# Attention followed by a gated projection on one core: heads paired as h and h+4, fewer loads, and projections issued as pairs of 128x64 column tiles

## The chip, the cores and the metric

The kernel runs on 1 core of one Trainium2 chip. The metric is the device time of one execution in microseconds (us), as the median of several executions. A profile of one execution shows every instruction of the five engines: TensorE (PE, whose weight loads are listed apart as PEld), VectorE (DVE), ScalarE (ACT), GpSimd (POOL) and SyncE (SP), which issues most of the transfers (DMAs).

## The reference

The inputs are q, k and v of shape 8 x 8 x 576 x 64 (batches, heads, tokens, head dimension, float32), a threshold tau, w_in (512 x 2048) and w_out (2048 x 512).

```python
scores = scale * np.matmul(q, k.transpose(0, 1, 3, 2))        # scale = 1/8
thresh = np.max(scores, axis=-1, keepdims=True) - tau
scores = np.where(scores >= thresh, scores, -1000000000.0)
attn   = softmax(scores)
x      = np.matmul(attn, v)          # heads side by side: 4608 tokens x 512
h      = x @ w_in
g      = h * np.clip(h + 3.0, 0.0, 6.0) / 6.0
out    = g @ w_out
```

## The kernel before, in words

**Slots.** Two heads make a pair, two pairs a quad; a batch has 8 heads, so two quads. A quad is done in nine slots: four slots of 128 queries for each pair, and a ninth (slot 8) with the last 64 queries of both pairs. 16 quads give 144 slots, numbered n. A slot computes for two heads at once a 128 x 576 table of scores, its row maximum, a mask, an exponential, its row sum, and the normalized probabilities in bf16, which are transposed into the tile pT (or pR for slot 8) by a DMA on SP, for the first slots by PE.

**The order is written out by hand.** Every engine runs its instructions in the order in which the loop over n (line 539) emits them. From slot 22 on (N1), slots come in twos, and PE does this:

- even slot: the first projection `mm1` (eight matmuls of 256 columns, line 394, or four of 512, line 389, for the rows that are left over of two batches), then eight matmuls of the second projection `mm2_part` (line 428, 512 columns);
- odd slot: `mm1` again, then, where the table `products` has one, a product of probabilities and v (`av`, lines 359 and 362: five steps, each a pair of matmuls), then the scores of two slots to come (line 295).

DVE does in every slot two maxima (line 310, which also copy the scores out of PSUM), a reciprocal (330) and the gate (417). In odd slots it also has the ReLU (404), the copy of the `av` result (370 or 380), every second time the copy of an output tile (436), and in some the transposition of a pair of q (245) or k (251). ACT does two masks (322) and two exponentials (327) in every slot, and the ReLU in even slots (402). POOL does the bias of the mask (317), the normalization (335), and issues the loads that change type.

**Shapes on PE.** A matmul of the scores contracts over 64 rows, since a head has 64 dimensions: the two heads of a pair lie on partitions 0 to 63 and 64 to 127 and use the two halves of the array's rows at once (in the profile 64\*128, rows by columns). A step of `av` is two matmuls of 128 rows by 64 columns (128\*64), one for each head, which write partitions 0 to 63 and 64 to 127 of the result. Projections and transpositions use the whole array (128\*128).

**Pairs and loads.** A pair is heads 2i and 2i+1. From batch 2 on (NB = 2) q and k are loaded by SP in blocks of 32 tokens by 32 dimensions, each piece 128 bytes, so that DVE can transpose them in 32 x 32 blocks (`blocks_q`, `blocks_k`, four DMAs for one pair). Of k the first 512 tokens go that way. The last 64 keys of a quad are loaded apart (tile kr, line 127, by POOL from quad 5 on), transposed by PE in an even slot (`transpose_rest`, line 261) and copied from PSUM by ACT in the odd slot after it (line 226, two copies). In kT the two heads of a pair lie in different column order, which is why line 294 adds 64 \* (1 - a).

**v.** Key tokens sit on the partitions of vm: 128 partitions of four tokens for the first 512, and the last 64 tokens in vr, whose other half is zero. An `av` step c takes one of the four tokens of each partition; the fifth step takes vr.

Of the kernel before, what the change touches and what calls it, by code (L numbers as in the profile page):

```python
# [9 lines left out]
F32 = mybir.dt.float32  # L10
# [10 lines left out]
def kernel(  # L21
# [60 lines left out]

    def load_quad(quad):
        b, g = divmod(quad, 2)
        nat[quad] = (nat_pool.tile([P, 1152], F32, tag="nq", name="nq"),
                     nat_pool.tile([P, 4, 4, D], F32, tag="km", name="km"),
                     nat_pool.tile([P, 2 * D], F32, tag="kr", name="kr"))
        nq, km, kr = nat[quad]

        def main(dst, src, h, order, by=nc.sync):  # L90
            by.dma_start(out=dst[:, :, h, :], in_=src[b, 4 * g + h, 0:512, :].rearrange(order, t=4))

        def blocks_q(n, a, j):
            c = 32 * (2 * a + j)
            nc.sync.dma_start(out=nq[c:c + 32, n * S:(n + 1) * S].rearrange("p (k d) -> p k d", d=32),
                              in_=q[b, 4 * g + 2 * n + a, :, 32 * j:32 * j + 32].rearrange("(k r) d -> r k d", r=32))

        def blocks_k(n, a, j):
            c = 32 * (2 * a + j)
            nc.sync.dma_start(  # L100
                out=km[c:c + 32].rearrange("p t h d -> p (t h d)")[:, n * 512:(n + 1) * 512].rearrange(
                    "p (t m d) -> p t m d", t=4, d=32),
                in_=k[b, 4 * g + 2 * n + a, 0:512, 32 * j:32 * j + 32].rearrange("(m r t) d -> r t m d", r=32, t=4))

        def load_k(n):
            if b < NB:
                for a in range(2):
                    main(km, k, 2 * n + a, "(p t) d -> p t d", by=nc.scalar if quad == n == 0 else nc.sync)
            else:
                for a in range(2):  # L110
                    for j in range(2):
                        blocks_k(n, a, j)

        def load_q(n):
            if b < NB:
                for a in range(2):
                    main(nq[:, 0:1024].rearrange("p (t h d) -> p t h d", h=4, t=4), q, 2 * n + a, "(t p) d -> p t d")
            else:
                for a in range(2):
                    for j in range(2):  # L120
                        blocks_q(n, a, j)

        def rest():
            for dst, src in ((kr[:], k), (nq[:, 1024:1152], q))[0:2 if b < NB else 1]:
                for n in range(2):
                    by = nc.scalar if quad == 0 and src is k else nc.sync if quad < 5 else nc.gpsimd
                    by.dma_start(out=dst[64 * n:64 * n + 64, :].rearrange("p (h d) -> p h d", h=2),
                                 in_=src[b, 4 * g + 2 * n:4 * g + 2 * n + 2, 512:S, :].rearrange("h p d -> p h d"))

        def both():  # L130
            rest()
            load_k(1)

        if b < NB:
            loads.extend((lambda: load_k(0), lambda: load_q(0), rest, lambda: load_k(1), lambda: load_q(1)))
        else:
            loads.extend((lambda: load_q(0), lambda: load_k(0), lambda: load_q(1), both))

    def load_v(b):
        vm = v_pool.tile([P, H, 4 * D], BF16, tag="vm", name="vm")  # L140
        vr = vrs[b % 2]
        vsb[b] = (vm, vr)
        w = 4 if b < NB else 2
        mains = [lambda h=h: nc.gpsimd.dma_start(  # L144
            out=vm[:, h:h + w, :], in_=v[b, h:h + w, 0:512, :].rearrange("h (p t) d -> p h (t d)", t=4))
            for h in range(0, H, w)]
        rests = [lambda a=a: nc.gpsimd.dma_start(
            out=vr[a * 64:(a + 1) * 64, a, :, :],
            in_=v[b, :, 512:S, :].rearrange("(hp a) p d -> a p hp d", a=2)[a]) for a in range(2)]
        vcasts.extend(mains + rests if b < NB else mains[0:1] + rests + mains[1:])  # L150


    vrs = []
# [6 lines left out]
    w_out_sb = singles.tile([P, NI, d_model], BF16)  # L160

    def load_weights():
        for n4 in range(4):
            for ki in range(KI):
                casts.append(lambda n4=n4, ki=ki: nc.gpsimd.dma_start(
                    out=w_in_sb[:, ki, n4 * 512:(n4 + 1) * 512],
                    in_=moe_w_in[ki * P:(ki + 1) * P, n4 * 512:(n4 + 1) * 512]))
        for ni in range(NI):
            casts.append(lambda ni=ni: nc.gpsimd.dma_start(
                out=w_out_sb[:, ni, :], in_=moe_w_out[ni * P:(ni + 1) * P, :]))  # L170
# [76 lines left out]
    def transpose_k(pair):  # L247
        if not by_pe(pair):
            n = pair % 2
            km = nat[pair // 2][1][:].rearrange("p t h d -> p (t h d)")  # L250
            nc.vector.transpose(out=kT_of(pair)[:, 64:576], in_=km[:, n * 512:(n + 1) * 512])
            return None
        pb = main_pe(nat[pair // 2][1], pair)
        return lambda: copy_out(kT_of(pair)[:, 64:576], pb)

    def transpose_rest(quad, of_k=True, of_q=True):
        pb = bank()
        nq, _, kr = nat[quad]
        of_q = of_q and by_pe(2 * quad)
        if of_k:  # L260
            nc.tensor.transpose(pb[:, 0:P], kr[:], identf[:])
        if of_q:
            nc.tensor.transpose(pb[:, P:2 * P], nq[:, 1024:1152], identf[:])

        def evict():
            qT, kT = qkT[quad]
            both = pb.rearrange("p (w n t) -> p w n t", n=2, t=64)
            if of_q:
                nc.vector.tensor_copy(out=qT[:, :, 512:S], in_=both[:, 1])
            if of_k:  # L270
                copy_out(kT[0:64, :, S:S + 64], both[0:64, 0])
                copy_out(kT[64:P, :, 0:64], both[64:P, 0])
        return evict
# [9 lines left out]
    def scores(n):  # L283
# [4 lines left out]
        for group in [((a,), parts) for a in heads] if n in (1, 2) else [(heads, (part,)) for part in parts]:  # L288
            for i in range(2 if slot == 8 else 1):
                for a, (k0, w) in [(a, part) for part in group[1] for a in group[0]]:  # L290
                    pair = 2 * quad + (i if slot == 8 else slot // 4)
                    rows = slice(64 * i, 64 * i + 64) if slot == 8 else slice(0, P)
                    q0 = 512 if slot == 8 else slot % 4 * P
                    c0, kc = score_col(n, a) + k0, 64 * (1 - a) + k0
                    nc.tensor.matmul(ps_flat[rows, c0:c0 + w],  # L295
                                     qT_of(pair)[a * 64:(a + 1) * 64, q0:q0 + rows.stop - rows.start],
                                     kT_of(pair)[a * 64:(a + 1) * 64, kc:kc + w], start=True, stop=True)
# [56 lines left out]
    def av(pb, pair, pT, cols):  # L354
        b, hp = divmod(pair, NPAIR)
        vm, vr = vsb[b]
        for c in range(4):
            for a in range(2):
                nc.tensor.matmul(pb[a * 64:(a + 1) * 64, :], vm[:, 2 * hp + a, c * D:(c + 1) * D],  # L359
                                 pT[:, 5 * a + c, cols], start=(c == 0), stop=False)  # L360
        for a in range(2):
            nc.tensor.matmul(pb[a * 64:(a + 1) * 64, :], vr[:, a, hp, :], pT[:, 4, cols], start=False, stop=True)  # L362
# [19 lines left out]

    def mm1(item, hb=HB):
        b, ni, c0 = item
        if c0 is None:
            for ki in range(KI):
                nc.tensor.matmul(ps[:, hb, :], xR[b // 2][:, ki, :], w_in_sb[:, ki, ni * P:ni * P + 512],  # L389
                                 start=(ki == 0), stop=(ki == KI - 1))  # L390
        else:
            for n in range(2):
                for ki in range(KI):
                    nc.tensor.matmul(ps[:, hb, n * 256:(n + 1) * 256], w_in_sb[:, ki, (ni + n) * P:(ni + n + 1) * P],  # L394
                                     xT[b][:, ki, c0:c0 + 256], start=(ki == 0), stop=(ki == KI - 1))
        return ps[:, hb, :]


# [25 lines left out]
    def mm2_part(bb, mt, part, ob=OB):  # L424
        if part == 0:
            o_ps[0] = ps[:, ob, :]
        for ni in range(part * 4, part * 4 + 4):
            nc.tensor.matmul(o_ps[0], gbuf[:, ni, mt * P:(mt + 1) * P], w_out_sb[:, ni, :],  # L428
                             start=(ni == 0), stop=(ni == NI - 1))

    def mm2_out(bb, mt, on_act):
        osb = o_pool.tile([P, d_model], F32, tag="osb", name="osb")
# [66 lines left out]
    for quad in range(1, NQUAD):  # L499
        n0 = quad * NSLOT  # L500
        first_odd = n0 - 9 + quad % 2
        for i, (job, of) in enumerate((("q", 2 * quad), ("k", 2 * quad), ("rest", quad),
                                       ("q", 2 * quad + 1), ("k", 2 * quad + 1))):
            turn_at(n0 + ((-5, -5, -4, -2, -1) if quad == 1 else (-6, -5, -4, -2, -1))[i] if quad < 3 else
                    first_odd + (0, 2, 3, 4, 6)[i] if quad > 3 else first_odd + (0, 2, 3, 5, 7)[i], job, of)

# [32 lines left out]
    for n, sl in enumerate(queue):  # L539
# [111 lines left out]
        elif n not in (4, 12, 15, 18, 21) and not 23 < n < 30 and (n < 37 or n % 2 == 0):  # L651
            start(loads, 1)
        if n < 4 or 15 < n < 20 or n > 33:
            start(vcasts, 1 if n < N1 or n % 2 else 0)
        else:
            start(casts, 2 if n in (5, 8, 11, 14) or 21 < n < 28 else 1)
        prev = sl
# [87 lines left out]
```

## Time and profile before

| | |
|---|---|
| median of 3 runs | 513.19 us (512.69 to 513.75) |
| span of the profiled execution, first to last instruction | 511.0 us |
| mean granted TensorE clock | 0.999 |
| DVE busy | 442.8 us (87%) |
| ACT busy | 450.3 us (88%) |
| POOL busy | 298.6 us (58%) |
| transposition of k by DVE, 128x512 (line 251) | 24 times, 704 ns |
| transposition of the last keys by PE (line 261) | 15 times |
| copies of the last keys by ACT, 64x128 (line 226) | 24 times, 253 ns |
| loads of the last keys by POOL (line 127) | 22 times, 632 ns |
| loads of q and of k by SP in blocks | 96 and 96, 72 KB and 64 KB, 3.4 and 3.2 us to landing |

The profiled execution has no time of its own beside its span; the runs' median lies 2.2 us above the span, which is the time around the first and last instruction. A group of the profile is named by its line, engine, operation, what it writes and reads, and how often it ran. Instructions on one engine overlap a little, so the distance from one start to the next is shorter than the duration that the profile gives; both are used below and told apart. Idle time is put down to what released the engine ("issue" means that nothing that the profile shows was waited for).

### The profile page before, as it was taken

What the parts mean: (1) busy time and instruction counts of PE and PEld (TensorE: products, weight loads), DVE (VectorE), ACT (ScalarE), POOL (GpSimd) and SP (SyncE); (2) the same over time, 40 slices, a digit from 0 to 9 for tenths busy, and PEclk for the clock granted to TensorE, in tenths of its full rate; (3) what the DMA queues carried; (4) which work ended last, traced back from release to release, by engine and by line L of the source; (5) the groups of instructions that cost most, each with busy time, mean ns of one, the idle gap of its engine ahead of it and who ended that gap; (6) DMA issues with size and microseconds to landing.
All of it is one profiled execution on the core that took longest, in us unless ns stands there. A gap on an engine that the chain in (4) does not pass through costs nothing.

```text
span 511.0 us, 12107 instructions
## 1 busy us (share of the span) xinstructions
PE 503.4 (99%) x4132; PEld 319.8 (63%) x4132; DVE 442.8 (87%) x1127; ACT 450.3 (88%) x977; POOL 298.6 (58%) x539
## 2 busy tenths in 40 slices
PE   8999999999999999999999999999999999999997
PEld 7656566666655666666655666666655666667564
DVE  4788899989999999999999999999999999887251
ACT  4999999999999999999999999999999999987160
POOL 2788879666666756656565656666566755552000
PEclk9999999999999999999999999999999999999999
DMA  6998999989999999999899999999999996563132
GB/s 144 182 172 147 153 143 182 174 157 178 188 160 172 163 174 160 205 162 181 150 158 181 154 163 163 179 169 175 163 178 149 187 177 116 114 111 75 72 57 77
DMA packets 314318, 78.77 MB, mean 154 GB/s; under 512 B 296880, under 2 KB 309424, under 8 KB 314256
## 3 DMA queue, kind: packets, MB, share of 16 engines
q1 hardware_dynamic: 294464, 67.90, 78.0%
q0 software_dynamic: 18304, 9.64, 15.6%
q8 instruction: 32, 0.52, 0.4%
q10 hardware_dynamic: 1488, 0.46, 0.4%
q14 instruction: 30, 0.25, 0.2%
HBM read 36.70 MB, written 9.44 MB: 90 GB/s over the span
## 4 chain that ended last, share of the span: by engine, by line
PE 80%; DVE 4%; ACT 3%; issue 1%; DVEq 0%
PE ps L295 24%; PE ps L428 23%; PE ps L394 20%; PE ps L359 7%; PE ps L389 3%; DVE s L310 1%; PE ps L362 1%; ACT s L327 1%; ACT s L322 1%; DVE g L417 1%; DVE r L404 1%; PE ps L668 1%; ACT r L402 1%; PE ps L350 0%; DVE xT L370 0%
## 5 line engine op out<-in xcount | busy, mean ns | idle before, releaser
L335 POOL TENSOR_SCALAR pn<-s,rinv 128x576 bf16<-128x576 f32 x288 | 210.6, 743 | 19.4 <-issue 4.8
L310 DVE TENSOR_SCALAR_CACHE_REDUCE s<-ps 128x576 f32<-128x576 f32 x288 | 205.0, 748 | 13.4 <-POOL pn L335 5.1
L322 ACT ACTIVATE s<-s,bias 128x576 f32<-128x576 f32 x288 | 205.7, 762 | 3.6 <-POOL bias L317 3.2
L327 ACT ACTIVATE s<-s 128x576 f32<-128x576 f32 x288 | 192.5, 671 | 0.3
L295 PE MATMUL ps<-kT,qT 64*128 64x384 f32 (+7 forms) x1280 | 175.5, 419 | 2.1 <-DVE s L310 2.0
L295 PEld LDWEIGHTS ps<-kT,qT 64*128 64x128 f32 (+1 forms) x1280 | 103.7, 175 | 57.8 <-issue 15.6
L394 PE MATMUL ps<-xT,w_in_sb 128*128 128x256 bf16 x1024 | 131.0, 273 | 0.6 <-DVE g L417 0.5
L428 PE MATMUL ps<-w_out_sb,g 128*128 128x512 bf16 x560 | 130.7, 379 | 0.0
L394 PEld LDWEIGHTS <-w_in_sb 128*128 128x128 bf16 x1024 | 95.6, 98 | 40.3 <-issue 21.0
L317 POOL TENSOR_SCALAR bias<-m 128x2 f32<-128x2 f32 (+1 forms) x147 | 27.5, 187 | 148.4 <-DVE rinv L330 132.1
L417 DVE SCALAR_TENSOR_TENSOR g<-r,ps 128x512 bf16<-128x512 f32 x128 | 87.8, 687 | 13.6 <-ACT r L402 9.1
L428 PEld LDWEIGHTS <-g 128*128 128x128 bf16 x560 | 54.6, 98 | 55.0 <-issue 0.4
L402 ACT ACTIVATE r<-ps,three 128x512 f32<-128x512 f32 x81 | 55.4, 686 | 25.1 <-PE ps L394 20.2
L327 ACT ACTIVATION_READ_ACCUMULATOR s<-s 128x1 f32 x288 | 54.5, 189 | 0.0
L404 DVE TENSOR_SCALAR r<-ps 128x512 f32<-128x512 f32 x63 | 42.9, 681 | 0.0
L359 PE MATMUL ps<-pT,vm 128*64 128x256 bf16 (+1 forms) x480 | 39.1, 285 | 0.0
L359 PEld LDWEIGHTS <-vm 128*64 128x64 bf16 x736 | 27.2, 110 | 16.1 <-issue 14.7
L370 DVE CAST xT<-ps 128x256 bf16<-128x256 f32 (+1 forms) x60 | 26.2, 437 | 10.2 <-PE ps L362 10.2
L436 DVE TENSOR_SCALAR osb<-ps 128x512 f32<-128x512 f32 x31 | 20.8, 672 | 8.4 <-PE ps L428 8.4
L310 DVE DVE_READ_ACCUMULATOR s<-ps 128x1 f32 x288 | 23.9, 83 | 0.0
L330 DVE RECIPROCAL rinv<-rsum 128x2 f32<-128x2 f32 x144 | 23.0, 160 | 0.7 <-ACT s L327 0.6
L144 POOL DMA_DIRECT2D vm<-in_v_dram x28 | 21.4, 766 | 0.1
(60 smaller groups left out, 256.6 us busy)
## 6 DMA issues: line engine op xcount, KB each, us to landing
out_dram<-osb SPq DMA_DIRECT2D x31, 256.0 KB, 2.6
nq<-in_q_dram SPq DMA_DIRECT2D x96, 72.0 KB, 3.4
km<-in_k_dram SPq DMA_DIRECT2D x96, 64.0 KB, 3.2
vm<-in_v_dram POOLq DMA_DIRECT2D x24, 128.0 KB, 3.9
nq<-in_q_dram SPq DMA_DIRECT2D x16, 128.0 KB, 4.9
w_in_sb<-in_moe_w_in_dram POOLq DMA_DIRECT2D x16, 128.0 KB, 3.7
w_out_sb<-in_moe_w_out_dram POOLq DMA_DIRECT2D x16, 128.0 KB, 4.1
pT<-pn SPq DMA_TRANSPOSE x117, 3.8
```

The lines of the kernel that those rows point to most:

```text
L295: nc.tensor.matmul(ps_flat[rows, c0:c0 + w], qT_of(pair)[a * 64:(a + 1) * 64, q0:q0 + rows.stop - rows.start], kT_of(pair)[a * 64:(a + 1) ...
L310: nc.vector.tensor_scalar(out=sl.s[:, i, :], in0=ps_flat[:, c0:c0 + S], scalar1=1.0, scalar2=None, op0=Alu.mult, op1=Alu.max, accum_out=sl ...
L317: nc.gpsimd.tensor_scalar(out=sl.bias[:, of], in0=sl.m[:, of], scalar1=-scale, scalar2=tau, op0=Alu.mult, op1=Alu.add)
L322: nc.scalar.activation(out=s, in_=s, func=Act.Prelu, bias=sl.bias[:, i:i + 1], scale=scale, alpha=REJECT)
L327: nc.scalar.activation(out=s, in_=s, func=Act.Exp, accum_out=sl.rsum[:, i:i + 1])
L335: nc.gpsimd.tensor_scalar(out=pn[:, i, :], in0=sl.s[:, i, :], scalar1=sl.rinv[:, i:i + 1], scalar2=1.0, op0=Alu.mult, op1=Alu.mult)
L359: nc.tensor.matmul(pb[a * 64:(a + 1) * 64, :], vm[:, 2 * hp + a, c * D:(c + 1) * D], pT[:, 5 * a + c, cols], start=(c == 0), stop=False)
L394: nc.tensor.matmul(ps[:, hb, n * 256:(n + 1) * 256], w_in_sb[:, ki, (ni + n) * P:(ni + n + 1) * P], xT[b][:, ki, c0:c0 + 256], start=(ki = ...
L402: nc.scalar.activation(out=r, in_=hps, func=Act.Relu, bias=three[:])
L404: nc.vector.tensor_scalar(out=r, in0=hps, scalar1=3.0, scalar2=0.0, op0=Alu.add, op1=Alu.max)
L417: nc.vector.scalar_tensor_tensor(out=out, in0=r, scalar=6.0, in1=hps, op0=Alu.min, op1=Alu.mult)
L428: nc.tensor.matmul(o_ps[0], gbuf[:, ni, mt * P:(mt + 1) * P], w_out_sb[:, ni, :], start=(ni == 0), stop=(ni == NI - 1))
```

## The change

Four things change together.

1. A pair is now heads h and h+4 of a batch. Which head lies where in xT changes with it, and the rows of w_in are loaded in the matching order: 8 DMAs of 64 x 4 x 512 in place of 16 of 128 x 512.
2. From batch 2 on, one DMA brings the blocks of two heads: 48 and 48 DMAs in place of 96 and 96, with pieces of 128 bytes as before. k is loaded whole (576 tokens), so there is no separate load, PE transposition or ACT copy of the last keys for these 12 quads. Token t of k is placed so that the keys of both heads come out in the same column order; DVE's transposition of k becomes two instructions (5 and 4 blocks of 64 columns). v is loaded in the matching order of tokens, in the same number of DMAs.
3. Every matmul of the projections is issued as two of 128x64, one for each half of the result's partitions, in all slots but the last. After the loop they are whole again.
4. The loads of v are given out a little differently (one in each slot below 40).

```diff
-        def blocks_k(n, a, j):
-            c = 32 * (2 * a + j)
-            nc.sync.dma_start(
-                out=km[c:c + 32].rearrange("p t h d -> p (t h d)")[:, n * 512:(n + 1) * 512].rearrange(
-                    "p (t m d) -> p t m d", t=4, d=32),
-                in_=k[b, 4 * g + 2 * n + a, 0:512, 32 * j:32 * j + 32].rearrange("(m r t) d -> r t m d", r=32, t=4))
+        def blocks(dst, src, a, order, **sizes):
+            rows = src[b, 4 * a + 2 * g:4 * a + 2 * g + 2].rearrange("n t d -> (n t) d")
+            for j in range(2):
+                c = 32 * (2 * a + j)
+                nc.sync.dma_start(out=dst[c:c + 32].rearrange("p (k d) -> p k d", d=32) if len(sizes) == 1 else
+                                  dst[c:c + 32].rearrange("p (t x d) -> p t x d", d=32, t=9),
+                                  in_=rows[:, 32 * j:32 * j + 32].rearrange(order, **sizes))
...
-            loads.extend((lambda: load_q(0), lambda: load_k(0), lambda: load_q(1), both))
+            loads.extend((lambda: load_q(0), lambda: load_k(0), lambda: load_q(1), lambda: load_k(1)))
...
-            km = nat[pair // 2][1][:].rearrange("p t h d -> p (t h d)")
-            nc.vector.transpose(out=kT_of(pair)[:, 64:576], in_=km[:, n * 512:(n + 1) * 512])
+            rows = nat[pair // 2][1][:].rearrange("p (t n w) -> p t n w", t=9, n=2)[:, :, n, :]
+            out = kT_of(pair)
+            for u in range(2):
+                e = 5 - u
+                nc.vector.transpose(out=out[:, 0:640].rearrange("p (c u w) -> p c u w", u=2, w=64)[:, 0:e, u, :],
+                                    in_=rows[:, 5 * u:5 * u + e, :])
...
+    def half_columns(out, lhsT, rhs, start, stop):
+        w = 64 if now < len(queue) - 1 else P
+        for c in range(0, P, w):
+            nc.tensor.matmul(out[c:c + w], lhsT[:, c:c + w], rhs, start=start, stop=stop)
+
     def mm1(item, hb=HB):
...
-                    nc.tensor.matmul(ps[:, hb, n * 256:(n + 1) * 256], w_in_sb[:, ki, (ni + n) * P:(ni + n + 1) * P],
-                                     xT[b][:, ki, c0:c0 + 256], start=(ki == 0), stop=(ki == KI - 1))
+                    half_columns(ps[:, hb, n * 256:(n + 1) * 256], w_in_sb[:, ki, (ni + n) * P:(ni + n + 1) * P],
+                                 xT[b][:, ki, c0:c0 + 256], start=(ki == 0), stop=(ki == KI - 1))
...
-            nc.tensor.matmul(o_ps[0], gbuf[:, ni, mt * P:(mt + 1) * P], w_out_sb[:, ni, :],
-                             start=(ni == 0), stop=(ni == NI - 1))
+            half_columns(o_ps[0], gbuf[:, ni, mt * P:(mt + 1) * P], w_out_sb[:, ni, :],
+                         start=(ni == 0), stop=(ni == NI - 1))
...
+            if job == "rest" and quad // 2 >= NB:
+                continue
```

More of the change, by code (lines that the diff above doesn't have):

```diff
@@ L84, in load_quad, with main @@
         b, g = divmod(quad, 2)
-        nat[quad] = (nat_pool.tile([P, 1152], F32, tag="nq", name="nq"),
-                     nat_pool.tile([P, 4, 4, D], F32, tag="km", name="km"),
-                     nat_pool.tile([P, 2 * D], F32, tag="kr", name="kr"))
+        nat[quad] = (nat_pool.tile([P, 2 * S], F32, tag="nq", name="nq"),
+                     nat_pool.tile([P, 2 * S], F32, tag="km", name="km"),
+                     nat_pool.tile([P, 2 * D], F32, tag="kr", name="kr") if b < NB else None)
         nq, km, kr = nat[quad]
-        def main(dst, src, h, order, by=nc.sync):
-            by.dma_start(out=dst[:, :, h, :], in_=src[b, 4 * g + h, 0:512, :].rearrange(order, t=4))
-        def blocks_q(n, a, j):
-            c = 32 * (2 * a + j)
-            nc.sync.dma_start(out=nq[c:c + 32, n * S:(n + 1) * S].rearrange("p (k d) -> p k d", d=32),
-                              in_=q[b, 4 * g + 2 * n + a, :, 32 * j:32 * j + 32].rearrange("(k r) d -> r k d", r=32))
-        def blocks_k(n, a, j):
-            c = 32 * (2 * a + j)
-            nc.sync.dma_start(
-                out=km[c:c + 32].rearrange("p t h d -> p (t h d)")[:, n * 512:(n + 1) * 512].rearrange(
-                    "p (t m d) -> p t m d", t=4, d=32),
-                in_=k[b, 4 * g + 2 * n + a, 0:512, 32 * j:32 * j + 32].rearrange("(m r t) d -> r t m d", r=32, t=4))
+        def main(dst, src, n, a, order, by=nc.sync):
+            by.dma_start(out=dst[:, 0:1024].rearrange("p (t h d) -> p t h d", h=4, t=4)[:, :, 2 * n + a, :],
+                         in_=src[b, 4 * a + 2 * g + n, 0:512, :].rearrange(order, t=4))
+        def blocks(dst, src, a, order, **sizes):
[5 more added lines that the diff above has]
+                                  in_=rows[:, 32 * j:32 * j + 32].rearrange(order, **sizes))
         def load_k(n):
@@ L107, in load_k @@
                 for a in range(2):
-                    main(km, k, 2 * n + a, "(p t) d -> p t d", by=nc.scalar if quad == n == 0 else nc.sync)
+                    main(km, k, n, a, "(p t) d -> p t d", by=nc.scalar if quad == n == 0 else nc.sync)
             else:
-                for a in range(2):
-                    for j in range(2):
-                        blocks_k(n, a, j)
+                blocks(km, k, n, "(x r t) d -> r t x d", r=32, t=9)
         def load_q(n):
@@ L116, in load_q @@
                 for a in range(2):
-                    main(nq[:, 0:1024].rearrange("p (t h d) -> p t h d", h=4, t=4), q, 2 * n + a, "(t p) d -> p t d")
+                    main(nq, q, n, a, "(t p) d -> p t d")
             else:
-                for a in range(2):
-                    for j in range(2):
-                        blocks_q(n, a, j)
+                blocks(nq, q, n, "(k r) d -> r k d", r=32)
         def rest():
-            for dst, src in ((kr[:], k), (nq[:, 1024:1152], q))[0:2 if b < NB else 1]:
+            for dst, src in ((kr[:], k), (nq[:, 1024:1152], q)):
                 for n in range(2):
-                    by = nc.scalar if quad == 0 and src is k else nc.sync if quad < 5 else nc.gpsimd
+                    by = nc.scalar if quad == 0 and src is k else nc.sync
                     by.dma_start(out=dst[64 * n:64 * n + 64, :].rearrange("p (h d) -> p h d", h=2),
[L128 to L132, printed above, removed]
+                                 in_=src[b].rearrange("(a n) t d -> n a t d", a=2)[2 * g + n, :, 512:S, :].rearrange(
+                                     "a p d -> p a d"))
         if b < NB:
@@ L142, in load_v, with tokens @@
         vsb[b] = (vm, vr)
[L143 to L150, printed above, removed]
+        if b < NB:
+            mains = [lambda h=h: nc.gpsimd.dma_start(
+                out=vm[:, h:h + 4, :], in_=v[b, h:h + 4, 0:512, :].rearrange("h (p t) d -> p h (t d)", t=4))
+                for h in range(0, H, 4)]
+            rests = [lambda a=a: nc.gpsimd.dma_start(
+                out=vr[a * 64:(a + 1) * 64, a, :, :],
+                in_=v[b, 4 * a:4 * a + 4, 512:S, :].rearrange("h p d -> p h d")) for a in range(2)]
+        else:
+            def tokens(a, first, count):
+                return v[b, 4 * a:4 * a + 4].rearrange("h (p t) d -> p h (t d)", t=9)[
+                    :, :, first * D:(first + count) * D]
+            mains = [lambda a=a, u=u, first=first: nc.gpsimd.dma_start(
+                out=vm[64 * u:64 * u + 64, 4 * a:4 * a + 4, :], in_=tokens(a, first, 4))
+                for a, u, first in ((0, 0, 0), (0, 1, 5), (1, 0, 5), (1, 1, 1))]
+            rests = [lambda a=a: nc.gpsimd.dma_start(
+                out=vr[a * 64:(a + 1) * 64, a, :, :], in_=tokens(a, 4 * (1 - a), 1)) for a in range(2)]
+        vcasts.extend(mains + rests)
     vrs = []
@@ L162, in load_weights @@
     def load_weights():
+        rows = moe_w_in.rearrange("(a ki d) f -> a d ki f", a=2, ki=KI)
         for n4 in range(4):
[L164 to L167, printed above, removed]
+            for a in range(2):
+                casts.append(lambda n4=n4, a=a: nc.gpsimd.dma_start(
+                    out=w_in_sb[64 * a:64 * a + 64, :, n4 * 512:(n4 + 1) * 512],
+                    in_=rows[a, :, :, n4 * 512:(n4 + 1) * 512]))
+                casts.append(lambda: None)
         for ni in range(NI):
@@ L249, in transpose_k @@
             n = pair % 2
-            km = nat[pair // 2][1][:].rearrange("p t h d -> p (t h d)")
-            nc.vector.transpose(out=kT_of(pair)[:, 64:576], in_=km[:, n * 512:(n + 1) * 512])
+            rows = nat[pair // 2][1][:].rearrange("p (t n w) -> p t n w", t=9, n=2)[:, :, n, :]
[4 more added lines that the diff above has]
+                                    in_=rows[:, 5 * u:5 * u + e, :])
             return None
-        pb = main_pe(nat[pair // 2][1], pair)
+        pb = main_pe(nat[pair // 2][1][:, 0:1024].rearrange("p (t h d) -> p t h d", h=4, t=4), pair)
         return lambda: copy_out(kT_of(pair)[:, 64:576], pb)
@@ L258, in transpose_rest @@
         nq, _, kr = nat[quad]
-        of_q = of_q and by_pe(2 * quad)
         if of_k:
@@ L293, in scores @@
                     q0 = 512 if slot == 8 else slot % 4 * P
-                    c0, kc = score_col(n, a) + k0, 64 * (1 - a) + k0
+                    c0, kc = score_col(n, a) + k0, (64 * (1 - a) if by_pe(pair) else 0) + k0
                     nc.tensor.matmul(ps_flat[rows, c0:c0 + w],
@@ L358, in av @@
             for a in range(2):
-                nc.tensor.matmul(pb[a * 64:(a + 1) * 64, :], vm[:, 2 * hp + a, c * D:(c + 1) * D],
+                nc.tensor.matmul(pb[a * 64:(a + 1) * 64, :], vm[:, 4 * a + hp, c * D:(c + 1) * D],
                                  pT[:, 5 * a + c, cols], start=(c == 0), stop=False)
@@ L388, in mm1 @@
             for ki in range(KI):
-                nc.tensor.matmul(ps[:, hb, :], xR[b // 2][:, ki, :], w_in_sb[:, ki, ni * P:ni * P + 512],
-                                 start=(ki == 0), stop=(ki == KI - 1))
+                half_columns(ps[:, hb, :], xR[b // 2][:, ki, :], w_in_sb[:, ki, ni * P:ni * P + 512],
+                             start=(ki == 0), stop=(ki == KI - 1))
         else:
@@ L653 @@
         if n < 4 or 15 < n < 20 or n > 33:
-            start(vcasts, 1 if n < N1 or n % 2 else 0)
+            start(vcasts, 1 if n < 40 or n % 2 else 0)
         else:
```

## The prediction

> **What bounds the kernel now.** I read the busy times first, then the chain that ended last, then the order of time on PE in two slots.
>
> ```profile
> PE 503.4 (99%) x4132; PEld 319.8 (63%) x4132; DVE 442.8 (87%) x1127; ACT 450.3 (88%) x977; POOL 298.6 (58%) x539
> ...
> PE 80%; DVE 4%; ACT 3%; issue 1%; DVEq 0%
> ```
>
> PE is busy for all but 7.6 us and makes most of the chain. A busy PE need not be at its peak, so the distances between starts count. This is PE's timeline, start and length in us, from an even slot to the next scores:
>
> ```profile
> 314.75 1.05 PE L394 MATMUL ps<-xT,w_in_sb 128*128 128x256 bf16 x8
> 315.64 1.89 PE L428 MATMUL ps<-w_out_sb,g 128*128 128x512 bf16 x8
> 317.36 1.04 PE L394 MATMUL ps<-xT,w_in_sb 128*128 128x256 bf16 x8
> 318.33 0.63 PE L359 MATMUL ps<-pT,vm 128*64 128x256 bf16 x8
> 318.79 0.28 PE L362 MATMUL ps<-pT,vr 128*64 128x256 bf16 x2
> 319.00 0.59 PE L295 MATMUL ps<-kT,qT 64*128 64x384 f32 x2
> ```
>
> Eight L394 before L428 take 0.89; before L359 they take 0.97, and L362's one pair takes 0.21 up to the scores. With the starts in ns: 109.2 from one L394 to the next, but 202.4 from the last L394 to the first L359 (50 times, all within 1 ns), 308 in place of 209 from scores to L394, 202 in place of 105 from L362 to the scores. A change of array shape costs 93 to 99 ns each time, and waits for nothing. Two slots hold three such changes. The second view is an earlier `av`, its first start and then, from a view that begins inside it, its third pair:
>
> ```profile
> 311.94 0.63 PE L359 MATMUL ps<-pT,vm 128*64 128x256 bf16 x8
> 312.40 0.28 PE L362 MATMUL ps<-pT,vr 128*64 128x256 bf16 x2
> ```
>
> ```profile
> 312.18 0.39 PE L359 MATMUL ps<-pT,vm 128*64 128x256 bf16 x4
> ```
>
> Two pairs in 0.22 us from 312.18 to 312.40: a pair of 128x64 tiles takes 109.2 ns (105.8 to the next pair, 3.4 within it), as one 128x128 matmul does. The first two took 0.24: the first pair after a change of shape takes 133, 24 more (start to start, all `av` of 256 columns). For 512 columns a pair takes 216, the first 236; for 64 columns 32, the first 53.
>
> **The change, part by part.** The compiled order of the new kernel gives the counts: 1376 projection matmuls become pairs (872 of 256 columns, 504 of 512).
>
> 1. Projections and `av` have one shape now: 59 of 61 changes into `av` go. 59 x 93.2 = 5.50 us.
> 2. Those `av` no longer start cold: 46 of 256 columns x 24 + 13 of 64 x 21 = 1.38 us.
> 3. The cold first pair goes to the projection after the scores instead: 54 x 24 + 7 x 20 = 1.44 us lost. The change of shape there stays.
> 4. The pairs themselves: 109.2 against 109.2 and 216 against 216. I take 0. Bounds: the mean of a whole step, with its hiccups, is 109.8 (872 x 0.6 = 0.5 us gained); if every pair took what a first pair takes, 872 x 24 + 504 x 20 = 31 us lost. I take 0 because pairs two to five of every `av` run at the lower figure.
> 5. The last keys' transpositions by PE: 12 x 109 = 1.31 us gained. They are in the stream, between L428 and L394.
> 6. Three turns of quad 3 (slots 22, 24, 26) still use 128x128 and now stand between other shapes: 6 x 94 + 3 x 24 = 0.64 us lost.
>
> PE's sum: -5.50 - 1.38 + 1.44 - 1.31 + 0.64 = **-6.1 us**. An ordinary two slots go from 6.39 to 6.30 us (93 saved; the 24 of points 2 and 3 cancel).
>
> What is late next? ACT is not: it loses 24 copies x 253 ns. From L428 to L394 the starts are 216 ns apart as a rule, but 315 six times and 244 to 257 five times, 0.8 us in all. At 310.98, one of the six, PE waits for the gate, the gate for ACT's ReLU, and that one came late behind the two copies in the slot before. Without copies I take 0.5 us as gained (ends 0 and 0.8). DVE is closest. Its rows, in a slot with k:
>
> ```profile
> 312.27 0.67 DVE L436 TENSOR_SCALAR osb<-ps 128x512 f32<-128x512 f32 x1
> 312.86 0.42 DVE L370 CAST xT<-ps 128x256 bf16<-128x256 f32 x1
> ...
> 314.51 0.70 DVE L251 STREAM_TRANSPOSE kT<-km 128x512 f32<-128x512 f32 x1
> 315.14 0.72 DVE L310 TENSOR_SCALAR_CACHE_REDUCE s<-ps 128x576 f32<-128x576 f32 x1
> ...
> 316.56 0.69 DVE L417 SCALAR_TENSOR_TENSOR g<-r,ps 128x512 bf16<-128x512 f32 x1
> ...
> 319.11 0.43 DVE L370 CAST xT<-ps 128x256 bf16<-128x256 f32 x1 [0.43 <-PE ps L362]
> ```
>
> k holds DVE for 0.627 (512 columns, start to start), q for 0.694 (576): 67 ns for 64 columns, so 94 ns are fixed. Two pieces of 320 and 256 then take 0.79: +0.161 each time, 3.9 us for 24. Ends: 0.067, the 64 columns alone, and 0.31, two whole durations (0.50 and 0.44 by the slope of the rows 704 and 771) that do not overlap. Behind them wait the maxima of the next slot, the even gate, and with it PE's odd `mm1`. The loop: `mm1` start to the next cast 319.11 - 317.36 = 1.75, now 1.63; cast to the gate's end 317.25 - 312.86 = 4.39; 0.05 to PE; +0.16: 6.23 us against PE's 6.30. So it is hidden by 0.07. Where the output copy (L436) stands ahead of the cast, as above, DVE came 0.13 late already (312.86 against 310.98 + 1.75 = 312.73) and PE comes 0.12 sooner: 6.23 + 0.25 = 6.48, 0.18 late. That is half of the 24, 2.2 us; with q in those places 6.23 - 0.16 + 0.07 + 0.25 = 6.39, 0.09 x 12 = 1.1 us. DVE gets back part of it in later slots (0.43 idle in the last line). With 0.31 in place of 0.161 it would be 12 x 0.08 + 12 x 0.33 + 1.1 = 6.0. Ends 0 and 6.0; I take **+1.2**, a little over a third of 2.2 + 1.1, since only a delay that lasts until the odd `mm1` counts.
>
> Loads: bytes are nearly the same. q of a pair needs both loads of q now, the third of four: quad 6 gets them in slots 36 and 40 and transposes in 45, five slots or 16 us later, with 3.4 us to landing. k waits for the fourth, slot 42, and transposes in 47. v is in by slot 39 for an `av` in 43. If this cover were gone, each of 12 quads would wait some 3 us. POOL loses 22 issues of 632 ns and 8 of w_in; it is at 58%. Slots before 22 and the end are as before. I take 0.
>
> Sum: -6.1 - 0.5 + 1.2 = **-5.4 us**. The profiled execution's span goes from 511.0 to 505.6; 2.2 us lie around it, so 513.2 becomes **507.8 us**.
>
> One rule speaks against point 4. The Trainium skill, "TensorE: Matmul & The Clock Gate", Part 3, says that a weight load overlaps running matmuls only where their row group differs; both column tiles use all rows. By that rule every pair would be a load and then its matmuls, an estimate of 110 ns more for each of 1376, and the sum would be near +146 us. The trace differs: in an `av` the two loads of the next pair start 2 and 5 ns after the running pair, last 110, and the next pair starts 109 after the last; L394 before the change does the same with whole loads of 98. The measurement decides.
>
> **The rivals.**
>
> *DVE becomes the bound.* For: it is busy 6.03 to 6.24 of 6.27 to 6.39 us in two slots with q or k. Against: the mean over such windows is 6.10. If the whole upper end reaches the path, 507.8 - 1.2 + 6.0 = 512.6 us; with k at 0.161 and nothing given back (3.3), 509.9, which I take as its time.
>
> *The 202 ns is no change of shape, but the wait of the first `av` load on its probabilities.* For: that load carries a semaphore wait each time. Against: the profile puts the weight loader's idle time before L359 (14.7 us, 63 times) down to "issue", so nothing awaited ended it, and 97 ns stand before the scores too. Then points 1 and 2 go: 507.8 + 6.9 = 514.7 us, or near 513.5 with DVE unstressed (its 1.2 gone).
>
> *Slower: the weight loads can't keep ahead in long runs.* An `av` is five pairs; the new kernel runs 29 in a row (8 + 8 + 8 + 5), with four instructions to a pair. Two windows in which PE and PEld have the most records (x) show (window, length, then busy time and records of PE, PEld, DVE, ACT and POOL):
>
> ```profile
> 453.90:460.20 6.30, 6.30 (x81) 4.14 (x82) 4.84 (x14) 4.84 (x12) 3.31 (x6) 1.00 0.79 138
> 447.50:467.50 20.00, 19.80 (x197) 14.21 (x197) 16.61 (x41) 16.45 (x36) 9.34 (x16) 1.00 0.56 103
> ```
>
> 163 in 6.3 us (39 ns each), but 394 in 20 us (51). The new kernel needs about 150 in every 6.3 us (42). If each pair then costs what a first pair costs, +31 us: 538.8 us. It decides from 5.4 us / 1376 = 4 ns a pair on.
>
> **How the numbers follow.** The forecast, 0.66. DVE as the bound, 0.13, still faster. No change of shape, 0.07, within 0.2% or a little over. Loads too slow, 0.14. A measurement of this kernel can tell about 0.2% (1 us) from no change. Faster 0.78 (the forecast and nearly all of the second case), same 0.07 (its worst and most of the third), slower 0.15. Low end: -6.1 - 0.8 - 0.5 = -7.4, 505.8, and 0.5 for the runs' scatter: 505.3. High end: the DVE case's worst, 512.6, and 0.5: 513.1. Above lie the fourth case and most of the third, 0.2 together.
>
> **What would show it.** Right: 109 ns from L394's last pair to the first `av` pair; scores to projection still 308; two slots at 6.30; k's two pieces at 0.79 from start to start; PE still at 98% or more. Wrong: pairs of 256 columns above 113 ns, PE waiting for the even gate in more than a third of its odd slots, or 202 ns before `av` as before.

## The result, and the profile after

The changed kernel takes 507.15 us (median of 4, 506.59 to 508.44) against 513.07 us before (4, 512.69 to 513.75). The ratio is 0.9886, with a 95% interval of 0.9874 to 0.9898. The span of the profiled execution went from 511.0 to 504.8 us, 6.2 us less; I had forecast 505.6 for the span and 507.8 for the time. Each run's time lies 1.8 us above its own span (506.59 and 504.8 for the profiled one); the 2.2 us that I took for the time around the first and last instruction were the distance of a median of three runs from the span of one.

These are the busy times and the chain that ended last, after:

```profile
PE 497.2 (98%) x5496; PEld 343.8 (68%) x5496; DVE 443.3 (88%) x1151; ACT 444.3 (88%) x953; POOL 279.9 (55%) x509
...
PE 81%; DVE 5%; ACT 1%; issue 1%; DVEq 0%
```

PE has 1364 more matmuls and as many more weight loads, and is busy 6.2 us less. Two slots of PE's timeline after, start and length in us; the six lines of before that the prediction shows are to be read against them (L393 is now both projections, L364 and L367 are `av`, L300 the scores):

```profile
291.89 1.06 PE L393 MATMUL ps<-xT,w_in_sb 128*64 128x256 bf16 x16
292.79 1.89 PE L393 MATMUL ps<-w_out_sb,g 128*64 128x512 bf16 x16
294.52 1.04 PE L393 MATMUL ps<-xT,w_in_sb 128*64 128x256 bf16 x16
295.39 0.60 PE L364 MATMUL ps<-pT,vm 128*64 128x256 bf16 x8
295.83 0.28 PE L367 MATMUL ps<-pT,vr 128*64 128x256 bf16 x2
296.03 2.21 PE L300 MATMUL ps<-kT,qT 64*128 64x384 f32 x16
```

The reader is to see three distances. From the second `mm1` to `av` (294.52 to 295.39) it is 0.87 us, eight pairs at 109 ns and nothing else; before, it was 0.97. The five pairs of `av` take 0.64 up to the scores, where they took 0.67. The first `mm1`, behind the scores, takes 0.90 up to `mm2` and took 0.89: it now has the cold first pair. From the last scores to the first tile it is 306 ns (308 before), where 209 would do without a change of shape: that one is still paid. An ordinary two slots take 6.28 us; they took 6.39, and I had forecast 6.30.

The second view is the slot with k on DVE, and PE's lines for the same time:

```profile
310.62 0.83 DVE L256 STREAM_TRANSPOSE kT<-km 128x320 f32<-128x320 f32 x2
311.38 0.72 DVE L315 TENSOR_SCALAR_CACHE_REDUCE s<-ps 128x576 f32<-128x576 f32 x1
...
312.79 0.67 DVE L427 SCALAR_TENSOR_TENSOR g<-r,ps 128x512 bf16<-128x512 f32 x1
```

```profile
311.70 1.89 PE L393 MATMUL ps<-w_out_sb,g 128*64 128x512 bf16 x16
313.50 1.06 PE L393 MATMUL ps<-xT,w_in_sb 128*64 128x256 bf16 x16
```

The two pieces hold DVE for 0.754 us from start to start (0.428 and 0.326). The gate ends at 313.46, and PE's `mm1` starts at 313.50, 1.80 us after `mm2` where 1.73 is usual (292.79 to 294.52): 75 ns of waiting. In the main stretch (110 to 450 us) this start is 12 to 77 ns late seventeen times, eight of them behind k (72 to 77 ns) and nine behind q (12 to 46), and each time an output copy came first on DVE. Together with one more, 80 ns at 116.8, that is 0.90 us.

### The profile page after: what moved, and what is told of

It reads as the page before. It is cut to its first block, busy times and chain, and to the rows that moved or that the text cites. A ratio compares the mean times of both kernels' runs of the same rounds, so it can differ in the third digit from the quotient of the medians.

```text
span 504.8 us, 14628 instructions
## 1 busy us (share of the span) xinstructions
PE 497.2 (98%) x5496; PEld 343.8 (68%) x5496; DVE 443.3 (88%) x1151; ACT 444.3 (88%) x953; POOL 279.9 (55%) x509
## 4 chain that ended last, share of the span: by engine, by line
PE 81%; DVE 5%; ACT 1%; issue 1%; DVEq 0%
PE ps L393 48%; PE ps L300 25%; PE ps L364 5%; DVE s L315 2%; PE ps L367 1%; DVE g L427 1%; DVE r L414 1%; PE ps L680 1%; ACT s L332 0%; ACT r L412 0%; PE ps L355 0%; DVE xT L375 0%; PE ps L238 0%; DVE kT L256 0%; DVE rinv L335 0%
## 5 line engine op out<-in xcount | busy, mean ns | idle before, releaser
L300 PE MATMUL ps<-kT,qT 64*128 64x384 f32 (+7 forms) x1280 | 175.7, 419 | 2.3 <-DVE s L315 2.1
L300 PEld LDWEIGHTS ps<-kT,qT 64*128 64x128 f32 (+1 forms) x1280 | 104.1, 175 | 57.7 <-DVE s L315 10.2
L393 PE MATMUL ps<-xT,w_in_sb 128*64 128x256 bf16 (+1 forms) x1896 | 132.5, 274 | 0.6 <-DVE g L427 0.6
L393 PE MATMUL ps<-w_out_sb,g 128*64 128x512 bf16 (+1 forms) x1016 | 130.9, 379 | 0.0
L393 PEld LDWEIGHTS <-w_in_sb 128*64 128x64 bf16 (+1 forms) x1896 | 108.1, 109 | 31.6 <-issue 21.9
L393 PEld LDWEIGHTS <-g 128*64 128x64 bf16 (+1 forms) x1016 | 61.5, 109 | 48.3 <-issue 0.4
L364 PE MATMUL ps<-pT,vm 128*64 128x256 bf16 (+1 forms) x480 | 38.5, 280 | 0.0
L364 PEld LDWEIGHTS <-vm 128*64 128x64 bf16 x736 | 32.7, 111 | 3.4 <-issue 1.4
L444 ACT ACTIVATE osb<-ps 128x512 f32<-128x512 f32 x4 | 2.4, 598 | 20.9 <-PE ps L393 14.6
```

Of the source, the lines that this page charges most:

```text
L300: nc.tensor.matmul(ps_flat[rows, c0:c0 + w], qT_of(pair)[a * 64:(a + 1) * 64, q0:q0 + rows.stop - rows.start], kT_of(pair)[a * 64:(a + 1) ...
L364: nc.tensor.matmul(pb[a * 64:(a + 1) * 64, :], vm[:, 4 * a + hp, c * D:(c + 1) * D], pT[:, 5 * a + c, cols], start=(c == 0), stop=False)
L393: nc.tensor.matmul(out[c:c + w], lhsT[:, c:c + w], rhs, start=start, stop=stop)
```

## The experiments

Every kernel ran beside the kernel before on the same chip; ratios are to that, with their 95% intervals.

**Whole matmuls, the rest of the change kept.**

```diff
-        w = 64 if now < len(queue) - 1 else P
+        w = P
```

> The changed kernel with the projections as whole 128x128 matmuls everywhere; pairing, loads and last keys stay as changed. Theory (the gain is changes of array shape on PE): points 1, 2, 3 and 6 of the prediction come back, 5.50 + 1.38 - 1.44 - 0.64 = 4.8 us, less 0.6 us of waits for DVE that a slower PE hides: 511.4 us; two ordinary slots take 6.39 us, 202 ns before av. Rival (the last keys and the halved loads carry the gain): 507 us. Rival (pairs of tiles are faster by themselves): 202 ns before av stays in both kernels.

511.06 us, ratio 0.995 (0.9932 to 0.9968). PE's timeline from `mm1` to `av`:

```profile
297.12 1.04 PE L393 MATMUL ps<-xT,w_in_sb 128*128 128x256 bf16 x8
298.09 0.63 PE L364 MATMUL ps<-pT,vm 128*64 128x256 bf16 x8
```

The 202 ns before `av` are back (all 55 places with 256 columns within 1 ns), and so 0.97 us in place of 0.87; the 308 ns after the scores are back too, and an ordinary two slots take 6.39. So the tiles are worth 3.9 us here by the medians (3.3 by the ratios, 4.5 by the spans, 509.3 to 504.8), and pairing, loads and last keys by themselves 2.3 us (513.36 to 511.06). That fits the 12 transpositions (1.3) and the gates that had waited behind ACT's copies: late starts of `mm1` cost 0.09 us here in the main stretch, where they cost 0.77 before. Pairing and loads were not run apart from the last keys.

**Tiles alone, on the kernel before.** `half_columns` is added as in the change, nothing else.

```diff
-                nc.tensor.matmul(ps[:, hb, :], xR[b // 2][:, ki, :], w_in_sb[:, ki, ni * P:ni * P + 512],
+                half_columns(ps[:, hb, :], xR[b // 2][:, ki, :], w_in_sb[:, ki, ni * P:ni * P + 512],
...
-            nc.tensor.matmul(o_ps[0], gbuf[:, ni, mt * P:(mt + 1) * P], w_out_sb[:, ni, :],
+            half_columns(o_ps[0], gbuf[:, ni, mt * P:(mt + 1) * P], w_out_sb[:, ni, :],
```

> The kernel before with the projections as pairs of column tiles up to the last slot; pairs of heads, loads and last keys as before. Theory: 59 changes into av go (-5.50 - 1.38), 61 cold pairs after scores (+1.44), but all 15 turns with whole transpositions of last keys or of quad 3 now stand between other shapes, 15 x (0.188 + 0.024) = +3.2: -2.3 us, 510.8 us. If the parts were independent, it would be what the tiles are worth in the changed kernel, -4.8 us: 508.3 us. Rival (the last keys carry the gain): 513 us.

517.96 us, ratio 1.0086 (1.0057 to 1.0115): slower than before, which none of the three expected. PE's own distances came out as reckoned (106 ns before `av` where nothing was awaited; 310 and some 259 ns on the two sides of a transposition of last keys, 216 and 109 before). What is new is this, on PE's timeline and in its list of waits (total us, times, longest):

```profile
169.42 0.60 PE L359 MATMUL ps<-pT,vm 128*64 128x256 bf16 x8
...
173.10 1.89 PE L388 MATMUL ps<-w_out_sb,g 128*64 128x512 bf16 x16
174.83 1.04 PE L388 MATMUL ps<-xT,w_in_sb 128*64 128x256 bf16 x16
179.51 1.06 PE L359 MATMUL ps<-pT,vm 128*64 128x256 bf16 x8 [3.65 <-DMA pT<-pn]
```

```profile
PE ps L359 <- DMA pT<-pn: 7.6, 5, 3.6
```

`av` waits for its transposed probabilities. On SP's queue, the same time:

```profile
168.50 2.43 SPq L95 DMA_DIRECT2D nq<-in_q_dram  x4
171.05 1.23 SPq L424 DMA_TRANSPOSE g<-go  x1
172.39 3.31 SPq L343 DMA_TRANSPOSE pT<-pn  x2
175.75 3.74 SPq L100 DMA_DIRECT2D km<-in_k_dram  x4
```

SP issues one transfer behind the other without a gap (in the 330 us from 110 to 440 its issues take 300 us; 284 in the kernel before, 292 in the changed one), and by the chain of waits the probabilities that were issued at 172.39 landed 7.1 us later, where 3.8 was the median before. The trace shows a second part, ahead of the issue: their normalization on POOL had ended at 164.88, so they stood for 7.5 us in SP's queue. All five products that waited had probabilities that stood there for 6.4 to 7.7 us; over the same 330 us the median of this wait is 3.3 us, and 1.5 in the kernel before.

Three such places (near 175, 358 and 412 us) lengthen the slots around them by 10.2 us in all. Without them the span would be 508.0; PE's terms gave 511.0 - 2.3 = 508.7. Not all of the 10.2 us is waiting (7.6): behind the longest wait PE was granted less clock. It was 1.00 in each 10 us from 110 to 170; the next two windows are these (window, length, busy time and records of PE, PEld, DVE, ACT and POOL, then the clock, and the share and rate of the DMA engines):

```profile
170.00:180.00 10.00, 6.35 (x74) 4.62 (x72) 5.71 (x15) 9.04 (x20) 5.17 (x11) 0.97 1.18 147
180.00:190.00 10.00, 10.00 (x98) 7.02 (x94) 8.14 (x19) 4.98 (x12) 5.51 (x10) 0.86 1.26 199
```

The eight matmuls of `av` at 179.51 took 1.06 us, where they took 0.60 at 169.42. The 3% and 14% that are missing from the clock are 1.7 us. The profiled execution was the longest of the four: their spans are 515.2 to 518.2, so the others lost less.

**Tiles in the first projection only.** `mm2_part` issues whole matmuls, the rest as changed.

```diff
-            half_columns(o_ps[0], gbuf[:, ni, mt * P:(mt + 1) * P], w_out_sb[:, ni, :],
+            nc.tensor.matmul(o_ps[0], gbuf[:, ni, mt * P:(mt + 1) * P], w_out_sb[:, ni, :],
```

> The changed kernel with tiles in the first projection only, whole matmuls in the second. Theory: every even slot then changes shape into the second projection and back, about 59 x (0.093 + 0.093 + 0.024) = +12.4 us: 519.5 us, slower than before, though fewer instructions are issued. Rival (a change of shape costs nothing, what counted was the tiles beside av or the instructions): 507 us or less.

518.1 us, ratio 1.0092 (1.0066 to 1.0118), and an ordinary two slots take 6.51 us, 0.23 over 6.28. The timeline shows the price after `mm2` (L438; one record of its eight is missing):

```profile
301.17 1.67 PE L438 MATMUL ps<-w_out_sb,g 128*128 128x512 bf16 x7 [0.16 <-issue]
302.77 1.06 PE L393 MATMUL ps<-xT,w_in_sb 128*64 128x256 bf16 x16
303.67 0.60 PE L364 MATMUL ps<-pT,vm 128*64 128x256 bf16 x8
```

From the last L438 to L393 it is 309 ns in place of 216 (49 times), and L393 to L364 0.90 in place of 0.87, the cold first pair. This is the clearest of the runs for the theory: with fewer instructions than the changed kernel the time is 11 us longer, and two changes of shape more in every two slots, with the cold pair behind them, account for it (0.23 us some 50 times).

**k in four pieces.**

```diff
-                e = 5 - u
-                nc.vector.transpose(out=..., in_=rows[:, 5 * u:5 * u + e, :])
+                for c0, e in ((0, 3), (3, 2 - u)):
+                    nc.vector.transpose(out=..., in_=rows[:, 5 * u + c0:5 * u + c0 + e, :])
```

> The changed kernel with k transposed by DVE in four pieces (3, 2, 3 and 1 blocks) in place of two, same columns. DVE holds 2 x 0.09 = 0.19 us more in 24 turns, 4.5 us in all. Theory (DVE has only 0.06 us to spare in these slots and none where the output copy comes first): 12 x 0.19 + 12 x 0.13 = 3.8 us at the most, half of it by slack later: +2 to +3.8 us, 509 to 511 us. Rival (DVE is hidden behind PE): 507.2 us.

509.09 us, ratio 0.9908 (0.9887 to 0.9928). By the medians that is 1.9 us over the changed kernel, by the ratios 1.1, and the two intervals overlap; the spans of the profiled executions are 506.5 and 504.8. The four pieces hold DVE for 0.87 us in place of 0.754, so they added 0.12 and not 0.19, 2.9 us in all. Between a third and two thirds of it reached the time. The traces say where: late starts of `mm1` cost 2.05 us in place of 0.90 in the main stretch. DVE is not hidden in these slots.

**q loaded by twice the DMAs.** In the changed kernel, `blocks` issues q for one head at a time.

```diff
+                    for n in range(2):
+                        nc.sync.dma_start(
+                            out=dst[c:c + 32, n * S:(n + 1) * S].rearrange("p (k d) -> p k d", d=32),
+                            in_=rows[n * S:(n + 1) * S, 32 * j:32 * j + 32].rearrange(order, **sizes))
```

> The changed kernel with q loaded by 96 DMAs of one head each in place of 48 of two; same bytes, same pieces of 128 bytes; k as changed. Tiles alone (the run before this one) lost 9 us to products that waited for their transposed probabilities, while SP's queue had no idle time. Theory (SP's queue of issues is close to full, and the halved loads keep it from being the bound): SP gets some 18 us more of issues in 330 us of the main stretch, of which it uses 292; stalls come back: +1 to +8 us, 508 to 515 us, with PE waiting for pT. Rival (the bytes, or POOL's loads of the last keys, made those stalls; or the prediction, which took the loads as free): 507.2 us, no wait for pT.

509.49 us (507.9 to 510.75), ratio 0.9927 (0.9903 to 0.9951), and PE waits for pT again:

```profile
PE ps L369 <- DMA pT<-pn: 2.3, 4, 1.3
```

So the loads were not free. The way was not the one that I expected: SP's issues from 110 to 440 take 294 us in place of 292, and not 18 more. But the probabilities stand longer in SP's queue, a median 3.3 us in place of 2.7, and the four that were late stood there for 6.2 to 7.6.

**Loads of the last keys kept on POOL.** `both` is, as before the change, `rest` (for k alone) and then `load_k(1)`.

```diff
-            loads.extend((lambda: load_q(0), lambda: load_k(0), lambda: load_q(1), lambda: load_k(1)))
+            loads.extend((lambda: load_q(0), lambda: load_k(0), lambda: load_q(1), both))
```

> The changed kernel which still issues the loads of the last keys on POOL (22 of 32 KB; nothing reads them, so the result does not need them). Theory (SP's queue was the cause of the stalls of tiles alone): 507 to 507.6 us. Rival (POOL's 0.63 us issues, which stand ahead of the normalization, made the probabilities late): several us more, with PE waiting for pT.

508.74 us (507.21 to 509.84), ratio 0.9912 (0.9886 to 0.9938), also with four waits for pT in the profiled execution, the longest of its four:

```profile
PE ps L368 <- DMA pT<-pn: 2.3, 4, 1.3
```

This speaks against the load of SP's queue as the only cause: SP issues what it does in the changed kernel (294 us and 292), its queue holds the probabilities no longer (a median 2.5 us and 2.7), and the waits are there. The four late ones had stood in it for 4.3 to 7.3 us and then took 4.2 to 6.6 to land. The run leaves open whether POOL's issues or the transfers that these loads add (22 of 32 KB) did it. Its interval overlaps the changed kernel's: two of the four executions (507.21 and 507.77 us) are as fast as that.

**Long pieces.** Both kernels load q and k in the same number of DMAs and the same bytes, but 2 to 4.6 KB of a partition at once; q and k then do not lie as the products need them, and only the amount of work is the same.

```diff
-            nc.sync.dma_start(out=nq[...].rearrange("p (k d) -> p k d", d=32),
-                              in_=q[b, h, :, 32 * j:32 * j + 32].rearrange("(k r) d -> r k d", r=32))
+            nc.sync.dma_start(out=nq[...],
+                              in_=q[b, h].rearrange("(r x) d -> r (x d)", r=32)[:, j * S:(j + 1) * S])
```

> Tiles alone (the kernel before with column tiles) whose 192 loads of q and k from batch 2 on keep their number, queue, order and bytes, but take each partition's 2 KB in one piece in place of 16 to 18 pieces of 128 bytes; the layout of q and k that DVE and PE then use is not the right one, the work is the same. Theory A (the DMA engines, which move small pieces slowly, were what made the probabilities late in tiles alone): no waits for pT, 510.5 us, the sum of PE's terms. Theory B (SP's queue is full because of the number of issues): the same 518 us. POOL's loads of the last keys are still there, so 518 would also fit them.

509.86 us (509.8 to 510.38), ratio 0.9937 (0.992 to 0.9953). With 216,025 packets in place of 314,329 the 8 us are gone; no wait for pT is left. The queue's share of the 16 DMA engines and the median from issue to landing, in tiles alone:

```profile
q1 hardware_dynamic: 294464, 67.90, 79.3%
```

```profile
pT<-pn SPq DMA_TRANSPOSE x117, 4.2
```

and with long pieces:

```profile
q1 hardware_dynamic: 196160, 67.90, 73.7%
```

```profile
pT<-pn SPq DMA_TRANSPOSE x117, 3.9
```

The number of DMAs alone was thus not the cause: the same number in long pieces leaves no wait. The larger part went through SP's queue: with long pieces SP's issue of a load of k is shorter (0.42 in place of 0.64 us), SP had 266 us to do in 330 in place of 300, and the probabilities stood in its queue for a median 0.8 us in place of 3.3. From issue to landing they gained only 0.3 us.

> The changed kernel with its 96 loads of q and k from batch 2 on in long pieces (4.6 KB) in place of 36 pieces of 128 bytes, same number, queue and bytes; the layout is not the right one, the work is the same. Theory A (the DMA engines are near their limit): pT lands sooner than 4.6 us, executions scatter less, 506.5 to 507 us, since PE waits for no transfer in the profiled execution of the changed kernel. Rival (transfers still take time from the changed kernel in most executions): 505.5 us or less.

506.68 us (506.53 to 507.32), ratio 0.9874 (0.9859 to 0.9889), span 504.8, as the changed kernel, though the transposes land in a median 3.9 in place of 4.6 us. The 4.6 us are more than the 4.2 of tiles alone, and yet no product of the changed kernel waits for pT: the median to landing by itself does not tell which kernel stalls. By the medians long pieces gain the changed kernel 0.5 us, and the intervals overlap: transfers cost it little.

**Tiles to the end.**

```diff
-        w = 64 if now < len(queue) - 1 else P
+        w = 64
...
-                nc.tensor.matmul(o_half, gbuf[:, ni, mt * P:(mt + 1) * P], w_out_sb[:, ni, columns],
+                half_columns(o_half, gbuf[:, ni, mt * P:(mt + 1) * P], w_out_sb[:, ni, columns],
```

> The changed kernel with column tiles in the last slot, in the matmuls after the loop and in the last tile's halves too. Theory: two changes of shape into av and two out of it go (4 x 0.093), one cold pair each: -0.3 us, within what can be told. Rival (tiles cost something where PE has no other work between: their later weight loads, or the gate and the copies that end the kernel): slower by 0.5 us or more, which would explain a limit at the last slot.

507.35 us, ratio 0.9891 (0.9875 to 0.9908), span 504.7. No difference that can be told; the limit at the last slot has no reason in these runs. No run beat the changed kernel beyond its interval.

## Why the prediction was right, point by point

- **Points 1 and 2, changes of shape (-5.50, -1.38).** Right, the mechanism and the size. The 202 ns before `av` became 78 to 106 wherever tiles of 256 columns stand before it, but for one place, and the whole-matmul run brought them back. The rival that these were waits for data is out.
- **Point 3, cold first pairs (+1.44).** Right: the first pair behind the scores takes 133 ns up to the next, as reckoned; 0.90 in place of 0.89 us in the timeline above.
- **Point 4, the pairs themselves (0).** Right, over 29 pairs in a row: 0.87 us for eight of 256 columns, 1.73 for eight of 512. They met the better one of my two bounds: of the whole matmuls of before 55 of 912 steps took 120 ns in place of 109, of the pairs none, which is the 0.5 us of the bound and most of the way from the forecast 6.30 us for two slots to 6.28. The weight loads (109 ns, 98 for whole ones) start beside the running pair, as in `av`. The slower rival falls with it. The rule of the Trainium skill that I weighed ("TensorE: Matmul & The Clock Gate", Part 3, loads overlap only in other row groups) is contradicted by this trace: two loads of 109 ns run beside the pair ahead of theirs, and pairs of 256 columns follow every 109 ns.
- **Points 5 and 6 (-1.31, +0.64).** They were not measured one by one. PE's sum was -6.1 and the span fell by 6.2, but with the 0.5 us of point 4 and the 0.1 of the next point the sum is -6.5, so 0.3 us stays without a place.
- **DVE (+1.2) and ACT (-0.5).** The mechanism was right, the size not. Late starts of `mm1` cost 0.77 us before, 0.09 with whole matmuls and no copies on ACT, and 0.90 after. So ACT's share went with its copies, and DVE's came with the faster PE, for the most part at the place that I named, k behind an output copy (0.60 us). I had 0.18 us for each of 12 and 0.09 for each of 12 with q; it was 0.075 for eight and 0.012 to 0.046 for nine. The two pieces take 0.754 and not 0.79, which is 0.04 of it; what gave the rest back was not looked into. Together the two terms should have been +0.1 and not +0.7, and that is most of the 0.8 us by which the span beat the forecast.
- **Loads, "I take 0".** Right for this kernel, but by luck as much as by reasoning. I costed the halving of the loads at nothing and looked only at q and k, which are early by slots. What comes late is another transfer on the same queue, the transposed probabilities. Tiles alone lost 10.2 us of span to it. In my price for "this cover gone" I named the wrong waiter. Nor did the halving empty the queue: from 110 to 440 SP issues the loads of q and k in 64 us in place of 104, but the transposes in 209 in place of 164, and the sum rises from 284 to 292. What led SP to take longer for each transpose was not tested.

## What to carry to other kernels

Where short groups of matmuls alternate, count how often the shape that PE runs in changes (rows by columns, transpositions included) and give neighbours one shape, even at twice the instructions: a change cost 93 to 99 ns here, a pair of 128x64 tiles no more than one 128x128 matmul of the same 256 or 512 columns. Change every group between them, or the price is paid twice. Before speeding up the engine that bounds, look at what has the least time to spare among the transfers, not only at those that the change touches: here transfers that SP's queue issued for 284 of 330 us turned a gain of some 3 us into a loss of 5.

## What the runs showed of the hardware that I had not expected

- Loads in pieces of 128 bytes hold up other transfers of the same core, and more ahead of their issue than behind it: with the same bytes in 2 KB pieces the probabilities stood in SP's queue for a median 0.8 in place of 3.3 us and landed 3.9 in place of 4.2 us after their issue, no product waited for them any more, and the time fell from 518.0 to 509.9.
- A wait of PE can cost more than its length: behind 3.65 us without work the granted clock was 0.86 over 10 us, and eight matmuls took 1.06 in place of 0.60 us.
- Two transpositions of DVE behind each other do not each cost the fixed 94 ns: the first piece does (0.428 - 5 x 0.067 = 0.093), the second only 0.326 - 4 x 0.067 = 0.058. With four pieces it is 0.094 for the first and 0.058 or 0.059 for each of the others.
- Behind each of the late starts of `mm1`, where no shape had changed, the pairs are split from the second one on, the second tile some 29 ns behind the first in place of 3; the next pair then follows sooner (80 in place of 106), and the 109 ns from pair to pair stay.
